# Hashed attention and a channel mix on one core: hints at a run-time branch, an earlier bound check, a store on another queue and a later mix

## The chip, the cores and the metric

The kernel runs on one core of a Trainium2 chip. The metric is the device time of one execution in microseconds (us). The time of the kernel before is the median of three runs. A profile shows one further execution: its *span* is the time from the first to the last instruction, and the execution's own time is somewhat longer than the span.

## The reference

Inputs are q, k and v of shape (4, 8, 768, 64): 4 batches, 8 heads, 768 tokens, head dimension 64. A 64 x 6 matrix `proj` hashes each token of q and k into one of 64 buckets. A token attends only to tokens of its own bucket. The result goes through a channel mix with two mixing vectors and three weight matrices.

```python
q_bits = einsum('bhsd,dk->bhsk', q, proj) > 0        # same for k
mask   = q_bucket[:, :, :, None] == k_bucket[:, :, None, :]
scores = where(mask, q @ k.T / 8, -1e9)
attn   = exp(scores - max) / sum
x      = attn @ v                                    # heads side by side: (4, 768, 512)
xk = mu_k * x + (1 - mu_k) * x_prev                  # x_prev: the token before
xr = mu_r * x + (1 - mu_r) * x_prev
out = sigmoid(xr @ w_r) * (relu(xk @ w_k) ** 2 @ w_v)
```

## The kernel before

The program has a fast path and a general path. The fast path (`fast`) does not subtract a row maximum. It appends the six hash bits to q and k as extra rows, so that a score of a foreign bucket comes out far below one of the same bucket, and takes the exp with a fixed offset. That is sound while the entries of q and k stay small. So the fast path also computes a bound: ScalarE squares q and k and sums the squares (`norm`, one Square pass with an accumulated sum for each pair and side), VectorE takes the largest sum of each partition (`nm`), TensorE transposes these by a product with the identity (`tps`), VectorE reduces them (`top`) and writes a flag (`check_bound`, lines 820 to 828). Behind the fast path each engine loads the flag into a register (line 997) and branches (line 998): if the bound does not hold, `general` computes everything again in a safe way. With the given inputs the bound holds, every engine jumps over the general code, and the program ends with waits for all semaphores and a barrier (lines 998 and 1025).

Heads are worked in pairs: 4 batches x 4 pairs = 16 pairs, n = 0 to 15. A pair has 12 *slots*: two heads times six blocks of 128 keys. In a slot, TensorE computes a block of scores (`score`, tile `sc`, two PSUM buffers of two banks each), ScalarE takes the exp (`pt`, line 458), and two slots later (`LAG = 2`) TensorE multiplies the exps with the values (`pv`, tile `oo`). The order of all instructions on each engine is written out by hand (`tc.manual_schedule`): what is emitted first in the Python code runs first on its engine.

Between the attention's instructions stand those of the channel mix of the batch before, taken from a queue of items (`ffn_items`, `ffn`): `kp` products with w_k (ReLU on ScalarE or VectorE into `kr`, square on VectorE into `k2`), `rp` products with w_r (tanh on ScalarE into `th`), and `vp` products with w_v, which VectorE multiplies by th + 1 into `os` (line 618); each `os` is stored to DRAM from SyncE's queue (line 622). How many items run in a slot is set by a rate, not by readiness. During attention the items use the two banks C and D in turn; after it, the four banks A, C, B and D.

When a pair is finished, `turn_out` transposes it into `xt`, and `mix` makes xk and xr of it in steps on VectorE: a difference `df` (line 521), a product with mu (line 525) and a sum (line 535).

Pairs n >= 6 (`NKEEP = 6`) have their two norms during attention, two pairs ahead, in slots 8 and 10 of pair n - 2 (line 303). So pairs 14 and 15 carry none. The first six pairs keep their q and k, and their 12 norms (line 295) are emitted in the last stage, the channel mix of batch 3, which runs alone after the attention: one norm in every second step x. The maximum `nm` follows at x = 26, `check_bound` at x = 32. Just ahead of that stage stand `turn_out` of pair 15, its two mixes (xk, then xr) and what is left of batch 2's vp items.

The last vp group of all is split into two halves of 256 columns (`parts` = 2, index `pt_`), so that the last store is half as large.

Of the kernel before, what the change touches and what calls it, by code (L numbers as in the profile page):

```python
# [31 lines left out]
def kernel(  # L32
# [13 lines left out]
    nc = tc.nc  # L46
    B, H, S, D = q.shape
# [7 lines left out]
    NPB = H // 2  # L55
# [117 lines left out]
    def fast():  # L173
        with ExitStack() as fx:
# [117 lines left out]
            def norm(n, i):  # L292
                junk = sqp.tile([P, S], BF16, name=f"sq{n}_{i}", tag="sq")
                if n < NKEEP:
                    nc.scalar.activation(
                        junk,
                        nats[n][:, i].rearrange("p j f -> p (j f)"),
                        AF.Square,
                        accum_out=nrm[:, i, n : n + 1],
                    )  # L300
                else:

                    nc.scalar.activation(  # L303
                        junk.rearrange("p (u d) -> p u d", u=NTOK),
                        blks[n][:, i, :, 0:32],
                        AF.Square,
                        scale=1.5,
                        accum_out=nrm[:, i, n : n + 1],
                    )
# [298 lines left out]
            def v_items(b, c, parts=1):  # L608
                sp, cc = divmod(c, 3)
                kcols = slice(cc * P, (cc + 1) * P)  # L610
                items = []
                w = DM // parts
                for pt_ in range(parts):
                    ms = slice(pt_ * w, (pt_ + 1) * w)

                    def done(vp, ms=ms, pt_=pt_):
                        os_ = osp.tile([P, w], FP32, name=f"os{b}_{c}_{pt_}", tag="os")
                        nc.vector.scalar_tensor_tensor(  # L618
                            out=os_, in0=mx["th", b, c][:, ms], scalar=1.0, in1=vp,
                            op0=ALU.add, op1=ALU.mult,  # L620
                        )
                        nc.sync.dma_start(
                            out=out[b].rearrange("(p c) m -> c p m", c=NC_)[c][:, ms], in_=os_
                        )

                    mms = [
                        (
                            lambda fc=fc: mx["k2", b, sp, fc][:, kcols],
                            lambda fc=fc, ms=ms: wv_sb[:, fc, ms],
                        )  # L630
                        for fc in range(NFC)
                    ]
                    items += [
                        (0.215 / parts, u)
                        for u in group([P, w], f"vp{b}_{c}_{pt_}", mms, done)
                    ]
                return items
# [17 lines left out]
            def ffn(amount):  # L655
                if not queue:
                    credit[0] = 0.0
                    return
                credit[0] += amount
                while queue and credit[0] > 0:  # L660
                    cost, u = queue.pop(0)
                    credit[0] -= cost
                    u()
# [76 lines left out]
            nslots = len(chunks)  # L740
            rate = 25.9 / (NPB * 12)
            heads = {}

            def oo_bank(n, j):
                return "AC"[j] if n < NPB else "AB"[j]
# [4 lines left out]
            for G in range(nslots + LAG):  # L750
                clock[0] = G
                n, s = divmod(G, 12)
                live = G < nslots
                run_due()

                if live and s == (6 if n == NPB - 1 else 3 if n == NPB else 1):
                    if n < NPAIRS - 2:
                        load_v(n + 2)
                    if n + 3 < NPAIRS:
                        (load_qk if n + 3 < NKEEP else load_blocks)(n + 3)  # L760
                w = weights.get(n, {}).get(s)
                if w:
                    load_w(*w)
                old = chunks[G - LAG] if G >= LAG else None
                first = old is not None and old[2] == 0
                if live:
                    score(*chunks[G])
                if old and not first:
                    pv(*old, oo_bank(*old[:2]))
                rate = 25.9 / (NPB * 12 + (3 if n >= NPAIRS - NPB else 0))  # L770
                ffn(rate / 2)
                mb = misc_bank(n, s)
                if live:
                    if G in first_block:
                        first_block[G]()

                    if s == (3 if n == 1 else 2) and 1 <= n < NKEEP - 1:
                        bits(n + 1, (0, 1), "B")
                    if s == 10 and NKEEP <= n + 2 < NPAIRS:
                        bits_blocks(n + 2, "A")  # L780
                    if s == 3 and n >= 1:
                        turn_out(n - 1, mb)
                    if n >= NPB:
                        if s == 4 and n % NPB == 0:
                            mix((n - 1) // NPB, (n - 1) % NPB, 0)

                        if s in (8, 9) and n % NPB:
                            mix((n - 1) // NPB, (n - 1) % NPB, 0, [(0,), (1, 2)][s - 8])
                    ms = (5, 7, 9)
                    if s in ms and 1 <= n < NPB:  # L790
                        mix(0, n - 1, 0, [ms.index(s)])

                    xs = [NPB * 12 + x for x in (5, 10, 11, 12)]
                    if G in xs:
                        mix(0, xs.index(G), 1)
                    if n > NPB and s == (10 if n % NPB else 5):
                        mix((n - 1) // NPB, (n - 1) % NPB, 1)
                    tn = (5, 7, 9, 11) if n == 1 else (4, 6, 8, 10)
                    if s in tn and 1 <= n < NKEEP - 2:
                        x = tn.index(s)  # L800
                        turn(n + 2, x % 2, x // 2, mb)
                    ts = (6, 7) if n % NPB == 0 else (4, 5)
                    if s in ts and NKEEP <= n + 2 < NPAIRS:
                        turn_blocks(n + 2, ts.index(s))
                    if n == 0 and s == 1:
                        values(0, 1)
                    vs_ = (8, 10) if n == 0 else (6, 9) if n < NPB else (0, 2)
                    if s in vs_ and n + 1 < NPAIRS:
                        values(n + 1, vs_.index(s))
                    if s in (8, 10) and NKEEP <= n + 2 < NPAIRS:  # L810
                        norm(n + 2, (s - 8) // 2)
                ffn(rate / 2)
                if old and first:
                    pv(*old, oo_bank(*old[:2]))
                if live and n >= NPB and n % NPB == 0 and s == MIXSLOT - 1:
                    queue.extend(ffn_items(n // NPB - 1))
# [3 lines left out]
            def check_bound():  # L820

                tps = ffbank([1, P], "tps")
                nc.tensor.matmul(tps, nm, ident32, start=True, stop=True)
                top = sgp.tile([1, 1], FP32, name="top", tag="top")
                nc.vector.tensor_reduce(out=top, in_=tps, axis=AX.X, op=ALU.max)
                nc.vector.tensor_scalar(
                    out=flag, in0=top, scalar1=8.0 * BOUND, scalar2=None, op0=ALU.is_le
                )
# [4 lines left out]
            def step():  # L833
                nonlocal G
                clock[0] = G
                run_due()
                G += 1
# [3 lines left out]
            step()  # L841
            turn_out(NPAIRS - 1, "B")
            mix(B - 1, NPB - 1, 0)
            mix(B - 1, NPB - 1, 1)
            while queue:
                ffn(rate)
                step()
            ffbanks[:] = ["A", "C", "B", "D"]
            ffnext[0] = 0
            queue.extend(ffn_items(B - 1))  # L850
            x = 0
            while queue:
                ffn(0.65)
                step()
                x += 1
                if x % 2 == 0 and x <= 4 * NKEEP:
                    norm((x // 2 - 1) // 2, (x // 2 - 1) % 2)
                if x == 4 * NKEEP + 2:
                    nc.vector.tensor_reduce(out=nm, in_=nrm, axis=AX.XY, op=ALU.max)
                if x == 4 * NKEEP + 8:  # L860
                    check_bound()
            step()

    def general():

# [127 lines left out]
        )  # L993

    with tc.manual_schedule():
        fast()
    ok = nc.values_load(flag[0:1, 0:1], min_val=0, max_val=1)
    with tc.If(ok == 0, preferred_fallthrough_block=True):
        general()


# [28 lines left out]
```

## Time and profile before

| | us |
|---|---|
| Median of 3 runs (lowest, highest) | 265.53 (265.42, 266.64) |
| The profiled execution | 266.43 |
| Its span | 264.6 |
| TensorE's products busy | 250.3 (95%) |
| VectorE busy | 180.0 (68%) |
| ScalarE busy | 216.1 (82%) |
| GpSimd busy | 123.0 (46%) |
| Granted clock of TensorE, mean | 0.995 |

In the profile's lines PE is TensorE (PEld its weight loads), DVE is VectorE, ACT is ScalarE, POOL is GpSimd and SP is SyncE. A letter q behind an engine (SPq, PEldq) means the engine's instruction queue: register, branch, semaphore and DMA-issuing instructions. L458 is line 458 of the kernel before. Starts are microseconds from the start of the span. In the lists of one line's instructions, the three numbers behind the count are the shortest, the median and the longest duration in nanoseconds, and "256.9 to 259.3" are the first and the last start. In the list of waits, the numbers are the total wait, how often, and the longest.

### The profile page before, as it was taken

What the parts mean: (1) busy time and instruction counts of PE and PEld (TensorE: products, weight loads), DVE (VectorE), ACT (ScalarE), POOL (GpSimd) and SP (SyncE); (2) the same over time, 40 slices, a digit from 0 to 9 for tenths busy, and PEclk for the clock granted to TensorE, in tenths of its full rate; (3) what the DMA queues carried; (4) which work ended last, traced back from release to release, by engine and by line L of the source; (5) the groups of instructions that cost most, each with busy time, mean ns of one, the idle gap of its engine ahead of it and who ended that gap; (6) DMA issues with size and microseconds to landing.
All of it is one profiled execution on the core that took longest, in us unless ns stands there. A gap on an engine that the chain in (4) does not pass through costs nothing.

```text
span 264.6 us, 6633 instructions
## 1 busy us (share of the span) xinstructions
PE 250.3 (95%) x2441; PEld 151.5 (57%) x2441; DVE 180.0 (68%) x377; ACT 216.1 (82%) x320; POOL 123.0 (46%) x251
## 2 busy tenths in 40 slices
PE   6999999998999999999999999998999999999990
PEld 5566656665565656565665656564656665455450
DVE  2675588769897766759587876778595746776440
ACT  3388879988999998979999998988999988079600
POOL 3669798695766472804574474607492000000000
PEclk9999999999999999999999999999999999999998
DMA  7923695976959291949575483959310002220132
GB/s 217 372 69 54 217 256 92 161 175 119 235 142 185 65 222 34 236 150 247 152 174 109 113 173 88 208 191 237 95 57 8 1 2 83 79 79 0 39 142 73
DMA packets 26488, 35.41 MB, mean 134 GB/s; under 512 B 3064, under 2 KB 22992, under 8 KB 26448
## 3 DMA queue, kind: packets, MB, share of 16 engines
q1 hardware_dynamic: 23936, 31.89, 46.4%
q0 software_dynamic: 2144, 2.62, 6.7%
q8 instruction: 21, 0.34, 0.6%
q10 hardware_dynamic: 368, 0.39, 0.5%
q14 instruction: 19, 0.16, 0.2%
HBM read 30.68 MB, written 6.29 MB: 140 GB/s over the span
## 4 chain that ended last, share of the span: by engine, by line
PE 72%; ACT 9%; DVE 7%; POOL 4%; DMA 2%; issue 2%; SPq 0%; ACTq 0%; DVEq 0%; POOLq 0%
PE sc L451 17%; PE vp L553 15%; PE kp L553 14%; PE oo L478 9%; ACT pt L458 8%; PE rp L553 7%; PE bb L369 3%; PE oo L469 2%; PE ot L503 2%; PE bb L409 1%; DMA vf<-in_v_dram 1%; DMA qk<-in_q_dram 1%; PE bdq L395 1%; DVE ob L490 1%; DVE kr L578 1%
## 5 line engine op out<-in xcount | busy, mean ns | idle before, releaser
L458 ACT ACTIVATE pt<-sc,expb 128x768 bf16<-128x768 f32 x192 | 167.7, 910 | 20.6 <-PE sc L451 18.6
L451 PE MATMUL sc<-aq,ak 70*128 70x384 bf16 x384 | 93.7, 325 | 1.8 <-ACT pt L458 0.7
L478 PEld LDWEIGHTS <-pt 128*128 128x128 bf16 x1152 | 60.5, 97 | 26.5 <-issue 0.2
L478 PE MATMUL oo<-va,pt 128*128 128x65 bf16 x1152 | 66.3, 193 | 0.0
L553 PE MATMUL kp<-xk,wk_sb 128*128 128x384 bf16 x256 | 55.7, 325 | 2.8 <-DVE kr L578 1.1
L553 PE MATMUL vp<-wv_sb,k 128*128 128x512 bf16 (+1 forms) x200 | 51.9, 370 | 0.0
L451 PEld LDWEIGHTS <-ak 70*128 70x128 bf16 x384 | 34.8, 98 | 27.6 <-issue 6.7
L586 DVE TENSOR_TENSOR k<-kr 128x384 bf16<-128x384 bf16 x64 | 27.1, 438 | 6.4 <-ACT kr L576 5.9
L553 PEld LDWEIGHTS <-wk_sb 128*128 128x128 bf16 x256 | 21.7, 97 | 14.3 <-issue 3.8
L353 POOL CAST aq<-tq 64x768 bf16<-64x768 f32 x20 | 16.5, 824 | 26.8 <-PE sc L451 11.7
L553 PE MATMUL rp<-wr_sb,xr 128*128 128x512 bf16 x96 | 28.9, 379 | 0.1
L576 ACT ACTIVATE kr<-kp 128x384 bf16<-128x384 f32 x36 | 18.1, 503 | 8.0 <-PE kp L553 8.0
L553 PEld LDWEIGHTS <-k 128*128 128x128 bf16 x200 | 16.7, 97 | 12.9 <-issue 2.7
L509 POOL COPY xt<-xt 128x127 bf16<-128x127 bf16 x12 | 3.5, 294 | 42.6 <-DVE xt L504 42.5
L439 POOL TENSOR_TENSOR s<-vf 128x192 f32<-128x192 f32 x32 | 22.7, 708 | 0.0
L618 DVE SCALAR_TENSOR_TENSOR os<-th,vp 128x512 f32<-128x512 bf16 (+1 forms) x25 | 16.5, 661 | 7.3 <-PE vp L553 5.4
L489 DVE RECIPROCAL rc<-oo 128x6 f32<-128x6 f32 x32 | 6.1, 191 | 21.9 <-PE oo L478 21.8
L578 DVE TENSOR_SCALAR kr<-kp 128x384 bf16<-128x384 f32 x28 | 15.4, 551 | 7.3 <-PE kp L553 7.1
L504 DVE COPY xt<-ot 128x768 bf16<-128x768 bf16 x16 | 8.9, 556 | 14.8 <-PE ot L503 14.8
L490 DVE TENSOR_TENSOR ob<-oo,rc 128x384 bf16<-128x384 f32 x32 | 17.8, 557 | 1.1
L355 POOL TENSOR_SCALAR ak<-tk 64x768 bf16<-64x768 f32 x20 | 16.6, 832 | 2.8 <-DVE tk L343 1.3
L303 ACT ACTIVATE sq<-blk 128x768 bf16<-128x768 f32 x20 | 17.0, 852 | 0.0
(83 smaller groups left out, 305.5 us busy)
## 6 DMA issues: line engine op xcount, KB each, us to landing
blk<-in_q_dram SPq DMA_DIRECT2D x40, 176.0 KB
blk<-in_k_dram SPq DMA_DIRECT2D x40, 176.0 KB
vf<-in_v_dram SPq DMA_DIRECT2D x16, 384.0 KB
out_dram<-os SPq DMA_DIRECT2D x23, 256.0 KB
qk<-in_q_dram SPq DMA_DIRECT2D x5, 384.0 KB
qk<-in_k_dram SPq DMA_DIRECT2D x5, 384.0 KB
wk_sb<-in_moe_w_k_dram POOLq DMA_DIRECT2D x2, 512.0 KB, 5.5
wv_sb<-in_moe_w_v_dram POOLq DMA_DIRECT2D x2, 512.0 KB, 5.8
```

Of the source, the lines that this page charges most:

```text
L303: nc.scalar.activation(junk.rearrange("p (u d) -> p u d", u=NTOK), blks[n][:, i, :, 0:32], AF.Square, scale=1.5, accum_out=nrm[:, i, n : n ...
L353: eng.tensor_copy(dst, src)
L355: eng.tensor_scalar(out=dst, in0=src, scalar1=ALPHA, scalar2=1.0, op0=ALU.mult, op1=ALU.mult,)
L439: nc.gpsimd.tensor_add(s3, vf[:, 0 : 3 * D], vf[:, 3 * D : 6 * D])
L451: nc.tensor.matmul(sc[:, sp, 0:HALF], au["k", j][:, jc * P : (jc + 1) * P], au["q", j][:, sp * HALF : (sp + 1) * HALF], start=True, stop=True,
L458: nc.scalar.activation(pt.rearrange("p (s q) -> p s q", s=2), sc[:, :, 0:HALF], AF.Exp, bias=expb, scale=SCALE,)
L478: nc.tensor.matmul(oo[:, ic, :], pts[n, j, jc][:, ic * P : (ic + 1) * P], vas[n, j][:, jc, :], start=False, stop=(jc == NC_ - 1 and ic == ...
L490: nc.vector.tensor_tensor(out=obs[n][:, :, j * D : (j + 1) * D], in0=oo[:, :, 0:D], in1=rc.to_broadcast([P, NC_, D]), op=ALU.mult,)
L553: nc.tensor.matmul(box["t"], lhs(), rhs(), start=(i == 0), stop=(i == len(mms) - 1))
L576: nc.scalar.activation(kr, kp, AF.Relu, scale=HALFROOT)
L578: nc.vector.tensor_scalar(out=kr, in0=kp, scalar1=0.0, scalar2=HALFROOT, op0=ALU.max, op1=ALU.mult,)
L586: lambda: nc.vector.tensor_tensor(out=k2, in0=kr, in1=kr, op=ALU.mult),
```

## The change

There are four parts.

- Eight of the twelve norms of the first six pairs move from the last stage into the attention of pairs 14 and 15, in slots 2, 5, 8 and 10; the remaining four stay in the last stage. The maximum is taken at x = 14 and the bound checked at x = 20.
- At x = 34, still inside the last stage, every engine loads the flag, and SyncE, VectorE, TensorE and ScalarE get a hint instruction for the branch. On TensorE the load and the hint stand within the fourth vp group of batch 3, on VectorE between its third and fourth os, on SyncE behind the third store. The branch itself is written for `held == 1` with an empty body, and the general path is its other side.
- The very last store (the second half of the split group) is issued from ScalarE's queue.
- The xr mix of pair 15 is emitted behind the rest of batch 2's items, so that on VectorE it follows the last two os of batch 2.

```diff
-                        nc.sync.dma_start(
+                        (nc.scalar if pt_ else nc.sync).dma_start(
                             out=out[b].rearrange("(p c) m -> c p m", c=NC_)[c][:, ms], in_=os_
                         )
...
+            kept = [(n, i) for n in range(NKEEP) for i in range(2)]
...
                     if s in (8, 10) and NKEEP <= n + 2 < NPAIRS:
                         norm(n + 2, (s - 8) // 2)
+                    if s in (2, 5, 8, 10) and n + 2 >= NPAIRS:
+                        norm(*kept.pop(0))
...
             mix(B - 1, NPB - 1, 0)
-            mix(B - 1, NPB - 1, 1)
             while queue:
                 ffn(rate)
                 step()
+            mix(B - 1, NPB - 1, 1)
...
-                if x % 2 == 0 and x <= 4 * NKEEP:
-                    norm((x // 2 - 1) // 2, (x // 2 - 1) % 2)
-                if x == 4 * NKEEP + 2:
+                if x % 2 == 0 and kept:
+                    norm(*kept.pop(0))
+                if x == 14:
                     nc.vector.tensor_reduce(out=nm, in_=nrm, axis=AX.XY, op=ALU.max)
-                if x == 4 * NKEEP + 8:
+                if x == 20:
                     check_bound()
+                if x == 34:
+                    held = nc.values_load(flag[0:1, 0:1], min_val=0, max_val=1)
+                    tc.mark_branch_hint_location(
+                        "bound", held, engines=[SP, DVE, PE, Activation])
             step()
+            return held
...
-        fast()
-    ok = nc.values_load(flag[0:1, 0:1], min_val=0, max_val=1)
-    with tc.If(ok == 0, preferred_fallthrough_block=True):
+        held = fast()
+    with tc.If(held == 1, preferred_fallthrough_block=False, label="bound") as fine:
+        pass
+    with fine.Else():
         general()
```

## The prediction

> **What bounds the kernel now.** I read the chain of waits first, on the page:
>
> ```profile
> PE 72%; ACT 9%; DVE 7%; POOL 4%; DMA 2%; issue 2%; SPq 0%; ACTq 0%; DVEq 0%; POOLq 0%
> ```
>
> TensorE carries the time, so an edit elsewhere counts only where it makes TensorE wait or where TensorE has finished. The change touches three such places. The first is the attention of the last two pairs (n = 14 and 15), which receive eight more Square passes on ScalarE. The timeline of ScalarE just before and inside that stretch shows what each of its operations costs:
>
> ```profile
> 196.30 0.91 ACT L458 ACTIVATE pt<-sc,expb 128x768 bf16<-128x768 f32 x1
> 197.08 0.61 ACT L595 ACTIVATE th<-rp 128x512 bf16<-128x512 f32 x1
> 197.56 0.92 ACT L458 ACTIVATE pt<-sc,expb 128x768 bf16<-128x768 f32 x1
> 198.34 0.87 ACT L303 ACTIVATE sq<-blk 128x768 bf16<-128x768 f32 x1
> 199.08 0.23 ACT L303 ACTIVATION_READ_ACCUMULATOR sq<-blk 128x1 f32 x1
> 199.17 0.93 ACT L458 ACTIVATE pt<-sc,expb 128x768 bf16<-128x768 f32 x1
> 199.95 0.53 ACT L576 ACTIVATE kr<-kp 128x384 bf16<-128x384 f32 x1
> ...
> 217.44 2.78 ACT L458 ACTIVATE pt<-sc,expb 128x768 bf16<-128x768 f32 x3 [0.59 <-PE sc L451]
> ```
>
> Columns: start, duration, engine, line. Read start to start, not the durations, which overlap: an exp occupies ScalarE 0.78 us, a tanh 0.48, a norm with its accumulator read 0.83, a ReLU 0.37. ScalarE is back to back here; later it waits for scores.
>
> The second place is the start of the last batch's output stage, in the chain and in the list of waits between 224 and 240 us:
>
> ```profile
> 225.98 0.18 PE oo L478 x6
> ...
> 230.60 0.66 PE kp L553 x4
> 231.26 0.06 issue
> 231.32 0.69 DVE os L618
> ```
>
> ```profile
> PE kp L553 <- DVE os L618: 0.8, 1, 0.8
> ```
>
> TensorE stops for 0.8 us because the second kp group needs the bank that an os operation still has to read, and that os sits on VectorE behind the two operations of the xr mix.
>
> The third is the end. TensorE's last product ends at 257.95 and the last os at 258.40, yet the span is 264.65. The instructions of the branch, and the store issues of SyncE between 256 and 260 us (durations in ns as min/median/max, then the first and last start):
>
> ```profile
> L998 SPq EVENT_SEMAPHORE  x8: 17/17/17, 262.5 to 263.0; - x8
> L998 PEldq COMPARE_BRANCH  x1: 3967/3967/3967, 256.3 to 256.3; - x1
> L998 DVEq COMPARE_BRANCH  x1: 72/72/72, 258.6 to 258.6; - x1
> L998 SPq COMPARE_BRANCH  x1: 45/45/45, 259.7 to 259.7; - x1
> L998 PEldq EVENT_SEMAPHORE  x1: 51/51/51, 260.3 to 260.3; - x1
> L998 DVEq EVENT_SEMAPHORE  x1: 21/21/21, 261.9 to 261.9; - x1
> ```
>
> ```profile
> L622 SPq DMA_DIRECT2D out_dram<-os x3: 333/383/1665, 256.9 to 259.3; - x3
> ```
>
> Each engine is silent for 2.7 to 4.0 us after its branch: SyncE 259.74 to 262.48, VectorE 258.62 to 261.93, TensorE 256.30 to 260.33. 16 KB of instructions travel for TensorE from 257.33 to 258.84 (queue q8 in the trace). SyncE's store issue begun at 257.55, in the middle of that, took 1.67 us instead of 0.33 and pushed the last issue to 259.31, 0.9 us after its data was ready. SyncE is the last to arrive: its rows from 262.48 on, 66 ns apart, and the final barrier end the span. By the trace the last store landed at 261.84, before SyncE looked.
>
> **Attention: eight norms moved from the tail (+2.85).** Pairs 14 and 15 had none; now each has four, at slots 2, 5, 8 and 10, and four remain in the tail. From the first exp of pair 14 (200.32) to where the last exp lets ScalarE go (224.63 + 0.78 = 225.41) are 25.09 us. In them ScalarE has 24 exps x 0.78, 3 ReLU x 0.37 and 3 tanh x 0.48 = 21.3 us, so 3.8 free. Eight norms x 0.83 = 6.6. The 27.9 us no longer fit, and the last exp ends 2.8 later. TensorE's last product of weights and values starts at 225.98, 0.44 after that exp's end at 225.54, where 0.05 would do (TensorE resumes at 232.05 after an os that ended at 232.00), so about 0.4 is absorbed: +2.4 is the floor. Everything behind it (turn_out, VectorE's mix, the remaining vp items) follows unchanged. Above the floor is what the two engines lose by waiting in turn, with two score buffers: pair 13 (186.14 to 200.32, 14.18 us) had 12 x 0.78 + 4 x 0.37 + 2 x 0.48 + 2 x 0.83 = 13.5 us of ScalarE work, so 0.7 unpacked, with TensorE also nearly full. Per pair that bounds the loss at 0 to 0.7; I take 0.45 for both, since ScalarE is now clearly the fuller one, and keep +2.4 to +3.8. The tail gains nothing by losing eight norms: from 232.05 to 247.14 the chain is TensorE without a break, whether ScalarE has norms or not.
>
> **The xr mix behind the output products (-0.80).** The two os operations run from about 230.4, end by 231.08 and 231.7, and the bank is free before kp's first group ends at 231.26. The mix (0.41 + 0.56) then ends near 232.65; its reader rp is third in line after three kp groups of 0.65, at 232.55, and needs this tile only with its fourth product, at 233.2. If that cover were gone it would give back 0.1 to 0.4. kr of the first group starts on VectorE at 232.5 as now. Bounds -0.8 and -0.5.
>
> **Bound checked sooner (0).** The max, the transposing product tps (0.31 on TensorE's chain), top and flag move from 249-253 to about 240-244 and cost the same there.
>
> **Loads of the flag and hints inside the stream (0).** TensorE's load (0.55 now at its end) and a hint stand two products before the end of the fourth last-batch vp group. Now the load runs at 255.62 while products run on to 257.95, so the queue is 2.3 us ahead and hides it. A hint is not in this trace; its nearest rows are SyncE's register operation, 0.19, and a branch, 0.05. Without the cover all of it costs 0.75; taken 0, kept 0 to +0.75. VectorE waits over 1.0 us for products there; SyncE's stores are 1.7 apart. The target's 16 KB for TensorE now travels some 4 us earlier and may hold a middle store 1.3 us, for which nobody waits.
>
> **The end (-1.75).** Let E be TensorE's last product; now the span ends at E + 6.70. ScalarE's queue, empty, waits for the last os (E + 0.45) and issues the store at E + 0.48; only its own branch is queued behind. SyncE issues the previous store at E - 0.40, branches at about E, and with its target already there stands at its semaphores before the data lands. So the landing becomes last: four comparable stores took 2.01 to 2.53 from issue start to landing; ScalarE's early load issues took 0.02 to 0.19 longer than SyncE's of the same size. I take 2.4: E + 2.9. From SyncE's second semaphore row, that store's, to the end were 2.07 us. E + 4.95, -1.75; bounds -2.1 and -1.4.
>
> **Sum.** 2.85 - 0.80 - 1.75 = +0.3. The profiled execution took 266.43 (span 264.6 and 1.8 around it), so 266.7; it lies 0.9 above the median of the three runs, 265.53, which gives **265.8**. Its own range from these bounds is 264.9 to 267.2. A measurement of this kernel can tell about 0.5%, 1.3 us, from no change.
>
> **Rivals.** *ScalarE and TensorE wait in turn (slower).* Place: pairs 14 and 15. Each norm holds up a score buffer, TensorE then stops before the next score and its output items do not fill the gap, as they stand behind that score. With pair 13's 0.7 per pair and no 0.4 absorbed, +4.2 - 0.8 - 1.75 = +1.65: 267.2. It decides slower once the attention loses over 3.9. For: pair 13. Against: TensorE has less to do in these two pairs. 0.18.
>
> *The hints fetch nothing.* Then SyncE, whose branch is earlier, still needs 2.74. TensorE, without a load in front, branches at E - 2.3, its 16 KB end near E + 0.2 and hold SyncE's store until E + 0.55, so SyncE arrives at E + 3.35 and ends 2.17 later: E + 5.5, the end gives -1.2 only, +0.85: 266.4. The trace has no hint to speak for or against it. The Trainium skill, Runtime: NRT & Kernel Launch, section Instruction fetch mechanics, states that instruction memory holds two lines and that prefetch is purely sequential, by which a hint could not keep a target and this time would hold. 0.13.
>
> *A hinted target displaces the block that comes next.* An engine that crosses a block before its branch then stops for up to 4.0 us less TensorE's 2.3 lead: +0.3 + 1.7 = +2.0: 267.5. Against: some 50 TensorE instructions stand between, and its last 16 KB block (256 instructions if 64 bytes each, an estimate from its 21 packets against some 5,000 instructions) came at 245.18. 0.03.
>
> *ScalarE absorbs the norms (faster).* If an exp's 0.78 were partly waiting for scores, the norms would fill that and the attention lose only 1.0: 1.0 - 0.8 - 1.75 = -1.55: 264.0. Against: no exp in the trace lets go before 0.78, not even the back-to-back ones. 0.08.
>
> The forecast has 0.58. Range 264.4 to 267.4: it drops the displaced block, most of the absorbing case and the forecast's outer tails. Faster by over 0.5%: 0.08 and little of the forecast = 0.10. Slower (over 266.86): 0.14 of waiting in turn, 0.03, and 0.05 from the upper ends of forecast and no-fetch = 0.22. Within: 0.68.
>
> **What would show it.** Last exp 2.4 to 3.8 later, ScalarE without idle time in pairs 14 and 15 and TensorE waiting at sc; the wait of kp for os gone; the branch rows of SyncE and VectorE followed by semaphore rows within 0.3 us, and the end near E + 5. Wrong: exps of pair 15 less than 2 us later, a gap of 2.7 us still behind SyncE's branch, or a new stop of TensorE among the last vp groups.

## The result, and the profile after

| | before | after |
|---|---|---|
| Median of 15 runs each, us (lowest, highest) | 266.08 (264.92, 267.34) | 267.52 (267.03, 268.95) |
| Ratio of the times, 95% interval | | 1.0067 (1.0049 to 1.0086) |
| Profiled execution, us | 266.43 | 267.03 |
| Its span, us | 264.6 | 265.2 |
| First exp of pair 14 to E, us | 57.63 | 59.62 |
| E to the end of the span, us | 6.70 | 6.27 |

The changed kernel is slower by 0.7%; 267.52 lies 0.12 above the range given. E is again the end of TensorE's last product: 257.95 before, 258.98 after. The two spans differ by only 0.6 us because the profiled execution of after happened to reach pair 14 0.96 us sooner (first exp at 199.36 instead of 200.32, in a part that the change does not touch). So all that follows is counted from that first exp or from E: 57.63 + 6.70 = 64.33 before, 59.62 + 6.27 = 65.89 after, a loss of 1.56.

The chain by engine, first line of its section on the page of after:

```profile
PE 55%; ACT 22%; DVE 8%; DMA 5%; POOL 4%; issue 3%; ACTq 0%; SPq 0%; POOLq 0%
```

ScalarE has 22% of the chain instead of 9%. The chain of after, its pieces from 220 us on (start, duration, what), shows where:

```profile
220.48 0.82 ACT sq L295 x2
221.31 2.38 ACT pt L458 x3
223.68 0.82 ACT sq L295 x2
224.50 1.40 ACT pt L458 x2
225.91 0.03 issue
225.93 0.98 ACT sq L295 x2
226.91 0.80 ACT pt L458
227.71 0.04 issue
227.75 0.36 PE oo L478 x6
```

Exps (pt) and moved norms (sq L295, each the Square and its accumulator read) follow one another without a gap up to the last exp. Only then can the last products of weights and values (oo) run. TensorE waits for it, in its own timeline, and no longer stops at kp:

```profile
227.75 0.36 PE L478 MATMUL oo<-va,pt 128*128 128x65 bf16 x6 [0.47 <-ACT pt L458]
...
232.38 2.15 PE L553 MATMUL kp<-xk,wk_sb 128*128 128x384 bf16 x12
```

The bracket is the idle time before a row and what ended it. The kp row has none: the 0.8 us wait for os is gone.

The end: the instructions of the branch (now on line 1015), and the last store issues on SyncE's and ScalarE's queues:

```profile
L1015 SPq EVENT_SEMAPHORE  x8: 17/17/17, 263.1 to 263.6; - x8
...
L1015 PEldq COMPARE_BRANCH  x1: 3774/3774/3774, 256.6 to 256.6; - x1
L1015 DVEq COMPARE_BRANCH  x1: 72/72/72, 259.0 to 259.0; - x1
L1015 SPq COMPARE_BRANCH  x1: 45/45/45, 259.4 to 259.4; - x1
L1015 ACTq COMPARE_BRANCH  x1: 62/62/62, 259.8 to 259.8; - x1
L1015 PEldq EVENT_SEMAPHORE  x1: 51/51/51, 260.5 to 260.5; - x1
L1015 DVEq EVENT_SEMAPHORE  x1: 21/21/21, 262.1 to 262.1; - x1
L1015 ACTq EVENT_SEMAPHORE  x1: 17/17/17, 263.2 to 263.2; - x1
```

```profile
L623 SPq DMA_DIRECT2D out_dram<-os x6: 332/332/737, 251.1 to 258.6; - x6
...
L623 ACTq DMA_DIRECT2D out_dram<-os x1: 361/361/361, 259.5 to 259.5; - x1
```

SyncE does branch 1.34 sooner (E + 0.45 instead of E + 1.79), and ScalarE issues the last store at once. But each of these engines is still silent after its branch: SyncE for 3.65 us, longer than the 2.74 of before, VectorE for 3.0, ScalarE for 3.3, and TensorE's branch takes 3.77. The hints brought no target. SyncE stands at its semaphores at E + 4.10, after the last landing (E + 3.70), and its rows and the barrier take 2.17 more.

### The profile page after: what moved, and what is told of

It reads as the page before. It is cut to its first block, busy times and chain, and to the rows that moved or that the text cites. A ratio compares the mean times of both kernels' runs of the same rounds, so it can differ in the third digit from the quotient of the medians.

```text
span 265.2 us, 6619 instructions
## 1 busy us (share of the span) xinstructions
PE 250.2 (94%) x2441; PEld 150.7 (57%) x2441; DVE 180.8 (68%) x377; ACT 215.7 (81%) x320; POOL 122.6 (46%) x251
## 4 chain that ended last, share of the span: by engine, by line
PE 55%; ACT 22%; DVE 8%; DMA 5%; POOL 4%; issue 3%; ACTq 0%; SPq 0%; POOLq 0%
ACT pt L458 16%; PE vp L553 12%; PE sc L451 12%; PE kp L553 10%; PE oo L478 7%; PE rp L553 6%; DMA qk<-in_k_dram 2%; ACT sq L295 2%; PE bb L369 2%; DMA ak<-sg 2%; PE ot L503 1%; PE oo L469 1%; PE bb L409 1%; ACT kr L576 1%; ACT sq L303 1%
## 5 line engine op out<-in xcount | busy, mean ns | idle before, releaser
L586 DVE TENSOR_TENSOR k<-kr 128x384 bf16<-128x384 bf16 x64 | 26.5, 430 | 5.6 <-ACT kr L576 5.2
L595 ACT ACTIVATE th<-rp 128x512 bf16<-128x512 f32 x24 | 14.9, 621 | 2.8 <-PE rp L553 2.8
```

The costliest lines, as they stand in the source:

```text
L586: lambda: nc.vector.tensor_tensor(out=k2, in0=kr, in1=kr, op=ALU.mult),
```

## The experiments

The theory after the result: attention and mix came out as summed, and the end failed because the hints fetched nothing. One candidate for why is the value they carry: the register `held` is 1 where the bound holds. The rivals: a hint cannot keep a target on this chip at all; or the loads, the hints or the second store queue cost something themselves. In the table, "first exp" is that of pair 14, "tail" is E to the end of the span; a gap runs from the start of a branch to the next row on that engine, for TensorE it is the branch's own duration.

| kernel | median, us | ratio to before (95%) | first exp to E | tail | SyncE gap | VectorE gap | ScalarE gap | TensorE branch |
|---|---|---|---|---|---|---|---|---|
| before | | | 57.63 | 6.70 | 2.74 | 3.31 | 2.87 | 3.97 |
| after | 267.52 | 1.0067 (1.0049 to 1.0086) | 59.62 | 6.27 | 3.65 | 3.04 | 3.34 | 3.77 |
| norms_only | 269.20 | 1.0112 (1.0077 to 1.0147) | 60.51 | 6.37 | 2.81 | 3.18 | 2.47 | 3.61 |
| mix_only | 264.99 | 0.9966 (0.9946 to 0.9986) | 56.71 | 6.39 | 2.77 | 3.31 | 2.89 | 3.67 |
| store_only | 264.99 | 0.9974 (0.9953 to 0.9995) | 57.63 | 6.53 | 3.06* | 3.79 | 3.26 | 3.64 |
| no_hint | 267.84 | 1.0064 (1.0039 to 1.0089) | 59.62 | 6.05 | 2.67* | 3.40 | 3.33 | 3.77 |
| hint_taken | 267.33 | 1.0050 (1.0031 to 1.0070) | 59.62 | 5.92 | 2.99 | 2.89 | 2.74 | 0.48 |
| hint_three | 267.67 | 1.0072 (1.0053 to 1.0092) | 59.62 | 5.90 | 3.28 | 0.61 | 3.14 | 3.77 |
| hint_many | 267.21 | 1.0055 (1.0032 to 1.0079) | 59.59 | 5.41 | 2.37* | 0.62 | 0.51 | 0.39 |
| four_norms | 265.23 | 0.9978 (0.9963 to 0.9993) | 57.45 | 5.86 | 3.23 | 3.34 | 2.87 | 0.49 |
| both_act | 264.25 | 0.9935 (0.9914 to 0.9957) | 56.71 | 5.74 | 2.90* | 3.27 | 3.35 | 3.59 |
| act_pool | 263.59 | 0.9909 (0.9890 to 0.9928) | 56.71 | 5.44 | 2.76* | 3.22 | 2.73 | 3.42 |
| both_pool | 263.41 | 0.9905 (0.9884 to 0.9927) | 56.71 | 4.70 | 0.50 | 2.92 | 2.69 | 3.77 |
| pool_hints | 264.62 | 0.9961 (0.9943 to 0.9979) | 56.71 | 4.90 | 0.53 | 0.62 | 0.51 | 0.39 |

Where a gap of SyncE is marked *, its first row stands 0.02 us behind the landing of the store that this row waits for (at E + 3.99 in store_only, 3.09 in no_hint, 3.03 in hint_many, 2.27 in both_act, 2.12 in act_pool). Such a gap ends with that landing, and the wait for instructions was at most as long.

### One part alone

**norms_only**: the kernel before with the norms moved and the bound checked sooner.

```diff
+                    if s in (2, 5, 8, 10) and n + 2 >= NPAIRS:
+                        norm(*kept.pop(0))
...
-                if x % 2 == 0 and x <= 4 * NKEEP:
-                    norm((x // 2 - 1) // 2, (x // 2 - 1) % 2)
+                if x % 2 == 0 and kept:
+                    norm(*kept.pop(0))
```

> The kernel before with one part alone: the eight norms moved into pairs 14 and 15, maximum at x = 14, bound checked at x = 20. Theory A, ScalarE has no room there: TensorE's last product 2.4 to 3.3 us later from the first exp of pair 14 on (2.8 from the changed kernel's shift of 2.0 plus the 0.8 of the mix), time 2.8 us over the kernel before, ratio 1.010. Rival B, ScalarE absorbs them: under +1.0 us, ratio under 1.004, and the changed kernel's shift of TensorE has another cause.

First exp to E is 60.51, 2.88 more than before. TensorE's timeline has both the late last products and the old wait at kp:

```profile
228.67 0.36 PE L478 MATMUL oo<-va,pt 128*128 128x65 bf16 x6 [0.46 <-ACT pt L458]
...
234.92 1.30 PE L553 MATMUL kp<-xk,wk_sb 128*128 128x384 bf16 x7 [0.80 <-DVE os L618]
```

Before, the last oo followed without a wait; here, as in after, it waits for the last exp. The norms' cost is the same 2.9 with or without the rest of the change.

**mix_only**: the kernel before with the xr mix behind the rest of batch 2's items, nothing else.

```diff
-            mix(B - 1, NPB - 1, 1)
             while queue:
                 ffn(rate)
                 step()
+            mix(B - 1, NPB - 1, 1)
```

> The kernel before with one part alone: the xr mix of pair 15 behind the rest of batch 2's items. Theory A: the 0.80 us wait of kp for os goes and nothing takes its place: 0.8 us less than the kernel before, ratio 0.997. Rival B: rp or kr waits for VectorE instead and 0.3 to 0.8 comes back: ratio 0.998 to 1.000, with a new wait of PE for xr or kr just behind.

First exp to E falls by 0.92: the first kp group to the second takes 0.69 instead of 1.61. In time this is a gain of 0.3%.

**store_only**: the kernel before with the very last store from ScalarE's queue.

```diff
-                        nc.sync.dma_start(
+                        (nc.scalar if pt_ else nc.sync).dma_start(
```

> The kernel before with one part alone: the very last store issued from ScalarE's queue. ScalarE then branches behind it, about 5 us later than in the kernel before. Theory A, fetches of jump targets that fall together hold each other up (the changed kernel's SyncE was silent 3.65 us, the kernel before's 2.74): SyncE silent about 3.6 us and the end about 7.1 us after TensorE's last product, 0.4 us slower than the kernel before. Rival B, each fetch takes its 2.7 us whatever the others do: SyncE branches 0.48 us earlier and the whole ends 0.5 us earlier, 6.2 us after the last product.

SyncE branches 0.84 sooner (E + 0.95), yet the tail is 0.17 shorter than before's and longer than those of norms_only and mix_only, which leave the tail's code as it was. ScalarE's branch, long past before (E - 3.96), now comes at E + 1.42, among the others, and the gaps of SyncE and VectorE are 3.06 and 3.79. SyncE's ends with the landing of its own store, the last but one, so it says nothing on theory A; VectorE's, 3.31 before, speaks for A. The end, E + 6.53, lies between A's 7.1 and B's 6.2, so neither is shown. The time, 0.26% below before, is more than this profile accounts for. That unchanged tails read 6.37, 6.39 and 6.70 also says how far one profile can be trusted: about 0.3 us.

### The hints

**no_hint**: the changed kernel without the hint instructions; the flag is still loaded at x = 34.

```diff
-                    tc.mark_branch_hint_location("bound", held, engines=[SP, DVE, PE, Activation])
```

> The changed kernel without the four hint instructions (the early flag load stays). Theory A, with the flag itself as the hint's value (1 where the bound holds) the hints ask for nothing: branch silences and the end after TensorE's last product (6.27 us in the changed kernel) the same within 0.3, time 267.5. Rival B, the hints do harm (an 8 KB instruction packet at 3.4 us before TensorE's end, a silence of SyncE of 3.65): without them the end is 0.7 us or more earlier, as in the kernel with the mix alone.

59.62 to E to the hundredth; the tail of 6.05 is 0.22 from after's, less than profiles of one tail differ; 267.84 us. The pages count as many instruction transfers with the hints as without: 21 on TensorE's queue q8, 19 on q14, which serves SyncE, VectorE and ScalarE. With the value `held` the hints do nothing, and they cost nothing that shows.

**hint_taken**: the changed kernel with the value turned round.

```diff
-                        held,
+                        1 - held,
```

> The changed kernel, with one edit: the hint's value is 1 - held, so 0 where the bound holds (the changed kernel passes held, which is 1 there). Theory A, the hint's sense was the wrong way round (0 asks for the jump's target, 1 does not): the silence after the branch of SyncE, 3.65 us in the changed kernel, and those of VectorE (2.96) and ScalarE (3.33) fall under 0.5 us; the landing of the last store becomes last, and the span ends 5.0 to 5.7 us after TensorE's last product instead of 6.26: 0.6 to 1.3 us less than the changed kernel (267.5), about 266.5. Theory B, no hint can keep a target in instruction memory: silences as in the changed kernel within 0.3 us, time the same. Theory C, the hint fetches but the block that comes next is displaced: a new stop of 2 to 4 us between hint and branch, time above 268.5.

The instructions of the branch:

```profile
L1015 PEldq COMPARE_BRANCH  x1: 484/484/484, 257.5 to 257.5; - x1
...
L1015 DVEq COMPARE_BRANCH  x1: 84/84/84, 259.9 to 259.9; - x1
L1015 SPq COMPARE_BRANCH  x1: 70/70/70, 260.6 to 260.6; - x1
...
L1015 DVEq EVENT_SEMAPHORE  x1: 21/21/21, 262.8 to 262.8; - x1
```

A new 16 KB instruction transfer for TensorE starts 1.2 us behind its hint, and its branch takes 0.48 instead of 3.77. So 0 is the value that asks for the target, and the change passes 1. That is shown for TensorE. On the other three engines no packet travels that no_hint lacks, and the gaps stay at 2.7 to 3.0, where theory A expected under 0.5: at this place the right value alone did not help them. TensorE is not the last to arrive, and the tail, 5.92, is little shorter than no_hint's 6.05. The time, 267.33, is not apart from that of after.

**hint_three**: the value turned round, hints on SyncE, VectorE and ScalarE alone, and six steps sooner.

```diff
-                if x == 34:
+                if x == 28:
...
-                        held,
+                        1 - held,
...
-                            mybir.EngineType.PE,
```

> The changed kernel with the hint's value turned round (1 - held), the hints given to SyncE, VectorE and ScalarE alone and 6 steps (some 4 us) sooner, at x = 28. A (the three hints came too late, or TensorE's 16 KB transfer took their place): instruction packets follow each hint within 1.5 us, the gaps behind these three branches fall from 2.7 to 3.3 us to under 0.7, the last landing (E + 2.9 to 3.7) becomes last and the span ends at E + 4.5 to 5.2; TensorE's branch takes 3.6 to 4.0 again; 266.1 to 266.8 us. B (a hint fetches nothing on these three engines): no packet follows the hints, the gaps stay at 2.7 to 3.4, the end at E + 6.0 to 6.3, 267.4 to 267.9 us.

Instructions of VectorE's branch:

```profile
L1014 DVEq COMPARE_BRANCH  x1: 84/84/84, 259.8 to 259.8; - x1
...
L1014 DVEq EVENT_SEMAPHORE  x1: 21/21/21, 260.4 to 260.4; - x1
```

VectorE goes on after 0.61 instead of 2.89. An 8 KB packet starts at E - 6.13, 1.7 behind VectorE's hint; the one at E - 3.42 that hint_taken and no_hint have is gone. In hint_taken VectorE's hint stood at E - 3.99, only 0.57 ahead of that packet. So on VectorE the place of the hint decides. That a sequential block (the next piece of the program, fetched in order), due within the transfer time, took its place is my reading and was not isolated. SyncE and ScalarE still waited (3.28 and 3.14), and SyncE sets the end: neither theory held whole.

**hint_many**: four hints on each engine, fixed at likely taken, so that they need no flag.

```diff
+                if x in (2, 10, 18, 26):
+                    tc.mark_branch_hint_location("bound", 0, engines=[SP, DVE, PE, Activation])
                 if x == 34:
                     held = nc.values_load(flag[0:1, 0:1], min_val=0, max_val=1)
-                    tc.mark_branch_hint_location("bound", held, engines=[SP, DVE, PE, Activation])
```

> The changed kernel with four hints on each of SyncE, VectorE, TensorE and ScalarE in place of one, each fixed at likely taken, at x = 2, 10, 18 and 26 (some 25, 20, 15 and 10 us ahead of E); the flag is still loaded at x = 34. A (a hint works on every engine where the engine stands at a suitable place of its instruction blocks, and VectorE's gap of 0.61 with the sooner hint was no accident): on ScalarE or SyncE too at least one hint is followed by an instruction packet within 2 us, and VectorE, TensorE and that engine go on within 0.7 us of their branches unless a later sequential block displaced the target. Then the end is set by the last landing, E + 4.9 to 5.6, 266.4 to 267.0 us. B (hints do nothing on SyncE and ScalarE): no packets behind theirs, gaps of 2.7 to 3.4 behind their branches, end at E + 5.7 to 6.1, 267.2 to 267.8 us.

The compiled program has the fixed hints at its very start, not at these steps. The hint instructions of TensorE, then those of the branch:

```profile
L1045 PEldq BRANCH_PREFETCH_HINT  x4: 31/31/50, 0.8 to 1.1; - x4
```

```profile
L1016 SPq EVENT_SEMAPHORE  x8: 17/17/17, 262.2 to 262.9; - x8
...
L1016 PEldq COMPARE_BRANCH  x1: 388/388/388, 256.8 to 256.8; - x1
...
L1016 SPq COMPARE_BRANCH  x1: 70/70/70, 259.9 to 259.9; - x1
L1016 ACTq COMPARE_BRANCH  x1: 76/76/76, 260.0 to 260.0; - x1
L1016 ACTq EVENT_SEMAPHORE  x1: 17/17/17, 260.6 to 260.6; - x1
```

Hints given 257 us ahead still serve: TensorE 0.39, ScalarE 0.51, VectorE 0.62. The instruction queues (transfers, MB, share of time) on the page of after, then on that of hint_many:

```profile
q8 instruction: 21, 0.34, 0.6%
q14 instruction: 19, 0.16, 0.2%
```

```profile
q8 instruction: 20, 0.33, 0.6%
q14 instruction: 16, 0.13, 0.2%
```

TensorE has one 16 KB transfer fewer. By this count the one at 244.43, where it has its sequential block in the other kernels, brought the target, as none follows until its branch at 256.85; what a transfer holds, the trace does not say. On q14 three 8 KB transfers are gone, where hint_three, which reached VectorE alone, has one fewer (18). So SyncE's hint served too, and its gap of 2.37 is not a wait for instructions: its first row, at E + 3.05, and its second, at E + 3.33, each stand 0.02 or less behind the landing that they wait for. The landing is last, as the prediction had wanted it, and the tail is 5.41. So theory A holds for ScalarE, by the count for SyncE, and for the tail (4.9 to 5.6); the median of 267.21 lies above A's 267.0, and its lowest run, the profiled one, is 266.38.

### Fewer norms, and the store

**four_norms**: the changed kernel, hint value turned round, with only four norms moved, all in pair 15; the maximum at x = 20 and the check at x = 26.

```diff
-                    if s in (2, 5, 8, 10) and n + 2 >= NPAIRS:
+                    if s in (2, 5, 8, 10) and n == NPAIRS - 1:
```

> The changed kernel with the hint's value 1 - held, and only four norms moved, all into pair 15 (slots 2, 5, 8, 10); the other eight stay in the last stage, maximum at x = 20, bound checked at x = 26. Theory A, what counts is ScalarE's room per pair (2.9 us free in pair 15, 1.0 in pair 14, start to start): four norms are 3.3, so TensorE's last product comes 0.0 to 0.5 later than without any, 2.4 to 2.9 us sooner than in the changed kernel; with a tail of about 5.9 the time is 1.2 to 1.8 under the kernel before, ratio 0.994. Rival B, each moved norm costs its share of the 2.9 us wherever it is put: four cost 1.4, ratio 0.998 to 1.000.

First exp to E is 57.45, 0.74 above mix_only's 56.71, where eight norms cost 2.91 (59.62). The chain of this kernel still runs through TensorE in pair 14 (where after's is ScalarE) and passes to ScalarE only at 216.83, in pair 15. So four norms cost 0.74 and eight cost 2.91: the first four found most of ScalarE's 3.8 us free, the next four added 2.2 of their 3.3 us to the path. The 0.74 lies between theory A (0.0 to 0.5) and rival B (1.4); A's ratio of 0.994 was missed, the time is 0.8 under the one before and not 1.2 to 1.8.

**both_act**: mix_only with both half-size last stores from ScalarE. **both_pool**: the same from GpSimd. **act_pool**: the first from ScalarE, the second from GpSimd.

```diff
-                        nc.sync.dma_start(
+                        (nc.scalar if parts == 2 else nc.sync).dma_start(                            # both_act
+                        (nc.gpsimd if parts == 2 else nc.sync).dma_start(                            # both_pool
+                        (nc.sync if parts == 1 else nc.gpsimd if pt_ else nc.scalar).dma_start(     # act_pool
```

> The kernel before with the xr mix moved as in the change, and both half-sized last stores issued from ScalarE. SyncE then branches right behind the store of vp group 4, about 0.6 us before TensorE's last product E. Theory A, the end is the last of three: SyncE's fetch (now done at about E + 2.2), the last landing (about E + 2.9) and 2.1 us of SyncE's rows behind it, and ScalarE's or VectorE's fetch (E + 4.0 to 4.4) and 0.9 behind that: end at E + 5.0 to 5.4 against 6.4 with the mix alone; time 1.9 to 2.2 under the kernel before, ratio 0.992. Rival B, the fetches of VectorE and ScalarE now hold up the landing or one another as with the last store alone: end at E + 6.0 or later, ratio 0.995 or more.

> As both_act, but both half-sized last stores issued from GpSimd, whose branch is followed at once by its next instruction (0.17 us in all runs) as it has no general code. ScalarE and SyncE branch before the end. Theory A, only VectorE still fetches late (E + 3.9) and the landing decides: GpSimd's issues took 0.71 to 0.94 us, 0.4 to 0.6 more than SyncE's, so the last landing is at E + 3.0 to 3.5 and the end at E + 5.1 to 5.6. Rival B, a store from GpSimd lands so much later than one from SyncE that the end is at E + 6.4 or later: no gain over the mix alone.

> The kernel before with the later xr mix, the first half-size last store from ScalarE's queue and the second from GpSimd's. A: GpSimd has no earlier store in front, so it issues at E + 0.48 instead of E + 0.75 as with both on GpSimd; the last landing comes 0.2 to 0.3 sooner, near E + 3.0, SyncE is back before it, and the span ends at E + 4.4 to 4.5: 263.1 us, 0.3 below both on GpSimd. B: ScalarE's branch now comes at about E instead of E - 4, its fetch meets those of SyncE and VectorE, and ScalarE or VectorE is last: gaps over 3.2 us, the end at E + 4.8 to 5.6, 263.5 to 264.3 us.

All three are faster than before by 0.65 to 0.95%. In all three SyncE branches at E - 0.62. In both_act ScalarE branches last of all, at E + 1.41, and is the last back, at E + 4.76, behind VectorE at E + 4.40: the tail of 5.74 lies between theory A's 5.4 and B's 6.0. In act_pool VectorE is last, at E + 4.33, as its theory B had it, with the tail (5.44) and the time inside B's numbers. In both_pool ScalarE's branch is at E - 3.96, out of the way, and SyncE's first row follows its branch after 0.50 us:

```profile
L998 SPq EVENT_SEMAPHORE  x8: 17/17/17, 256.7 to 259.5; - x8
...
L998 SPq COMPARE_BRANCH  x1: 50/50/50, 256.2 to 256.2; - x1
...
L998 DVEq COMPARE_BRANCH  x1: 72/72/72, 257.5 to 257.5; - x1
L998 POOLq COMPARE_BRANCH  x1: 45/45/45, 258.4 to 258.4; - x1
...
L998 DVEq EVENT_SEMAPHORE  x1: 21/21/21, 260.4 to 260.4; - x1
```

But SyncE still waits. Its eight rows run from 256.7 to 259.5: 2.27 us lie between the third and the fourth, though the store that the fourth waits for had landed 8 us before. In the list of SyncE's waits (total, how often, longest) both stand together, 0.50 and 2.27, and behind them the wait for GpSimd's last store:

```profile
SPq L998 <- SPq L998: 2.7, 2, 2.3
...
SPq L1025 <- DMA out_dram<-os: 0.3, 1, 0.3
```

It branches early enough to be through by E + 2.34, ahead of the last landing at E + 3.24. both_act does not differ from this on SyncE as far as its rows show: its 2.90 ends with the landing of ScalarE's first store. GpSimd issues a store in 0.55 to 0.64 instead of SyncE's 0.33 and goes on 0.17 behind its branch in every kernel. The tail of 4.70 is shorter than theory A's 5.1 to 5.6, though the landing came as expected: the row that waits for GpSimd's last store is the twelfth of SyncE's and not the second, so that 1.44 us of rows and barrier stand behind it instead of 2.07. act_pool's second store started at E + 0.75, not at the E + 0.48 that was expected: GpSimd does not issue at once. both_pool, 263.41, beats both kernels; act_pool, 263.59, is not apart from it.

**pool_hints**: both_pool with one fixed hint on each of the four engines.

```diff
-    with tc.If(ok == 0, preferred_fallthrough_block=True):
-        general()
+    with tc.If(ok == 1, preferred_fallthrough_block=False, label="bound") as fine:
+        pass
+    with fine.Else():
+        general()
```

> The kernel before with the later xr mix, both half-size last stores from GpSimd's queue, and one hint on each of SyncE, VectorE, TensorE and ScalarE, fixed at likely taken, which the compiler puts at the program's start. A (the hints arm the branch targets): TensorE, VectorE and ScalarE go on within 0.7 us of their branches as they did with four hints, TensorE's 16 KB no longer travel while the last stores are under way, SyncE is back before the landing, and the last landing, E + 2.9 to 3.2 against E + 3.24 with both stores on GpSimd and no hint, sets the end 1.5 to 1.7 later: E + 4.4 to 4.8, 263.1 to 263.5 us. B (SyncE, which went on in 0.50 without a hint, now waits for its block again, as one instruction more at the start shifts its blocks): SyncE's gap 2.4 to 3.0, back at about E + 2.3, the end E + 4.8 to 5.4, 263.5 to 264.1 us.

All four engines go on within 0.62 us, SyncE also without the stop of 2.27 behind its third row, and the tail is 4.90: as in both_pool the landing (E + 3.44) decides, and it did not come sooner than the E + 3.24 there. The hints did on every engine what A says, and the time is outside both theories. The median, 264.62, lies 1.2 above both_pool's. The tail explains 0.2 of that; the rest is unexplained (before's own runs beside it were 0.6 lower than beside both_pool). In time the hints gain nothing here.

## Why the prediction was wrong, step by step

- **Attention, +2.85 taken: 2.88 (norms_only) and 2.91 (after against mix_only).** Right, also in its parts: the last exp ends 28.34 us after the first of pair 14 instead of 25.21, 3.13 later; the last products of weights and values start 2.90 later. Between the last exp's end and those products lay 0.29 before (225.53 to 225.82), not 0.44, and 0.05 after, so 0.24 was absorbed instead of 0.4; waiting in turn cost 3.13 - 2.8 = 0.33 instead of 0.45. The two misses cancel, so that the last 0.1 us of the agreement is luck.
- **The xr mix, -0.80 taken: -0.92.** Right; a little better than the bound.
- **The bound sooner, loads and hints in the stream, 0 taken.** No row of TensorE stops for them: after, no_hint and hint_taken agree at 59.62.
- **The end, -1.75 taken: -0.43. This is the step that failed**, and with it the sum: 2.90 - 0.92 - 0.43 = 1.55, against +0.3. Two of its assumptions broke. "With its target already there" was false. The hint carried 1 where 0 asks for the target (TensorE's branch: 3.77 and 0.48), and at this place 0 brought SyncE nothing either (2.99 in hint_taken); only the hints at the program's start served there. And the landing was put 2.4 behind the issue: it took 3.22 in after and 2.84 in hint_many. The trace of before had two stores at 3.46 and 4.07, issued at 256.94 and 257.55, which the four called comparable left out. The end of hint_many is its landing, E + 5.41. By it the missing targets cost 6.27 - 5.41 = 0.86 and the late landing 5.41 - 4.95 = 0.46, together the 1.32 missed. By after's own landing (E + 3.70, and 2.07 behind it E + 5.77) they cost 0.50 and 0.82. Each tail is good to 0.3 only, so which of the two is the larger stays open.
- **The rival that the hints fetch nothing** had the mechanism, at 0.13, with the end too low (E + 5.5). Its branch time was nearly right (E + 0.45 for 0.55), but the gap that it took from before, 2.74, became 3.65. In after, VectorE, SyncE and ScalarE all branch between E + 0.04 and E + 0.87, and their three packets start at E + 1.19, 1.46 and 1.82. That these hold each other up was not isolated, and in no_hint, where the three branch at the same times, SyncE was back after 2.67 at most, a microsecond sooner. The Trainium skill, Runtime: NRT & Kernel Launch, section Instruction fetch mechanics, says that a taken branch out of the window forces a fetch of the target before execution goes on; the gaps of 2.5 to 4.0 without a hint agree. Its purely sequential prefetch does not hold here: a hint brought TensorE's branch from 3.77 to 0.39.
- **The base.** The prediction started from 265.53, the median of three runs; beside the changed kernel the one before took 266.08. Of the 1.72 between 265.8 and 267.52, 0.55 is this and the rest, 1.17, nearly all of the sum's error of 1.25. The range drawn from the bounds was too narrow as added up: they allow from 2.4 - 0.8 - 2.1 = -0.5 to 3.8 - 0.5 + 0.75 - 1.4 = +2.65, so 265.0 to 268.2 and not 264.9 to 267.2, and 267.52 lies inside.
- **Waiting in turn** did not come at the rival's size, 2.9 against 4.2: TensorE stopped at sc for 0.7 us, in two waits. **ScalarE absorbing the norms** did not happen. The displaced block did not arise in after, whose hints fetched nothing.

What stays open: why hints with the value 0 in the last stage brought SyncE (2.99 to 3.28) and ScalarE (2.74 to 3.14) nothing in hint_taken, hint_three and four_norms, while hints at the program's start served both, and why SyncE has the first three rows behind its branch at once in both_pool.

## What to carry to other kernels

A price from a back-to-back row (a norm 0.83 on ScalarE, start to start) against the engine's free time forecast a stage to 0.1 us; an assumed state of the machine at the end (a target that is already there) and a landing put too early were the whole error. Give each such state its own test in the trace, and read the sense of an instruction's operand before counting on it. Before a gap behind a jump is put down to instructions, look for what the next row waits for: in five of the fourteen kernels SyncE's gap ended with a landing. Where several engines end with a far jump, look for the one that both stores last and jumps last: moving the last stores to an engine whose jump is cheap here (GpSimd, 0.17) gained more than hints did.

## What the runs showed of the hardware that was not expected

- A branch hint on a register acted at value 0 (TensorE in hint_taken, VectorE in hint_three) and did nothing at 1 (after). Its cost is 0.03 to 0.06 us. Fixed at 0 and given at the start of a 264 us program, a hint was still good at the end (hint_many, pool_hints).
- A branch whose hint served took 0.4 to 0.6 us until the next row, one without 2.5 to 4.0 where no landing ended the gap, on GpSimd 0.17. The exception is SyncE in both_pool: 0.50 without a hint, and 2.27 more behind its third row.
- A hint 4.0 us ahead of E brought nothing on VectorE, and one 7.8 us ahead did.
- The last store of 256 columns took 2.1 to 3.2 us from issue start to last landing when it came from ScalarE's queue (both_act 2.12, store_only 2.18, hint_taken 2.40, hint_many 2.84, after 3.22), so the 2.4 taken needed some 0.8 above it.
